# Attention in padded head pairs, fp32 transposes on TensorE, interleaved batches, and a hand-written TensorE order across two MoE layers

## The chip, the cores and the metric

The kernel runs on one core of a Trainium2 chip. The metric is device time in microseconds (us), the median of several runs. TensorE is PE in the profile (its weight loads PEld), VectorE is DVE, ScalarE is ACT, GpSimd is POOL, SyncE is SP. L171 is line 171 of the kernel concerned; before and after have their own numbers.

## What is computed

Four batches of 768 positions pass a linear attention with a decaying state per head (8 heads, 48 channels each), and its output, as x of 3072 x 384, a mixture of four experts in which every expert sees every row.

```python
for t in range(S):
    kt, vt, rt = (k[:, :, t].copy(), v[:, :, t].copy(), r[:, :, t].copy())
    cur = np.einsum('bhd,bhe->bhde', u[None] * kt, vt)
    y[:, :, t] = np.einsum('bhd,bhde->bhe', rt, state + cur)
    state = w[None, :, :, None] * state + np.einsum('bhd,bhe->bhde', kt, vt)
...
p = domain_probs / (domain_probs.sum(-1, keepdims=True) + 1e-09)
for e in range(E):
    h = np.maximum(x @ w1[e], 0.0)
    out += p[:, e:e + 1] * (h @ w2[e])
```

r, k, v, w and u are fp32, w1 is 4 x 384 x 1024 and w2 4 x 1024 x 384; the output is fp32.

## The kernel before

The work is cut into 24 chunks of 128 positions, six per batch, batch after batch. For a chunk `attn_chunk` (L118 to L191) loads r, k and v with positions on partitions (SP's queue, L126 to L128, three buffers each). VectorE multiplies r and k by powers of the decay into bf16 (L131, L133). GpSimd makes Khat, k scaled for the state (L135), Vb, v in bf16 (L137), the two products r·k·u (L140, L141), and, when VectorE has summed them per head (dcoef, L143), dv, the part of the position itself (L145).

TensorE transposes r and k head by head, 8 + 8 bf16 transposes of 48 columns (L149, L155), which VectorE copies out of PSUM (L151, L157). A per head is a product over 48 rows (L164); VectorE masks it to the triangle in two halves (AtM, L166). Y is, per head, AtM times Vb over 128 positions and r times the state over 48 rows, in turns (L171, L173). VectorE adds dv (Ysb, L176). The state's increment St is Khat times Vb per head (L180), after which VectorE decays the state and adds (L182, L184). Three transposes (L189) and a copy (L191) bring the chunk's Y, with its 384 channels on partitions, into xTe, which holds four chunks.

The MoE takes groups of four chunks. For each of 6 groups and 4 experts, 24 slots in all, layer 1 has 8 blocks of 128 hidden units, three matmuls of 512 columns each (L229), which ScalarE rectifies into hTs (L234); layer 2 has four blocks, one per chunk, of 8 matmuls of 384 columns (L238). VectorE scales a block by the expert's weight into tmp (L242), and GpSimd adds it to the accumulator oacc (L244), which it has cleared (L221). Four output DMAs on SP's queue follow a group (L248).

Six chunks are issued ahead of the MoE, then one at the start of every slot until they are used up (`issue_chunk`). The weights come in two DMAs of 3 MB each on GpSimd's queue, issued after the first chunk. Within this order of issue a scheduler decides how the instructions lie on each engine. PSUM has two buffers for transposes and A (tag trps), two for Y and St, two for layer 1 and two for layer 2.

## Time and profile before

| | us |
|---|---|
| runs | 437.08, 436.20, 436.51; median 436.51 |
| the profiled execution: span | 435.5 |
| TensorE busy | 370.9 (85%), 2568 matmuls |
| GpSimd busy | 215.9 (50%) |
| VectorE busy | 205.9 (47%) |
| ScalarE busy | 122.0 (28%) |
| moved by DMA | 25.62 MB |

The span runs from the first to the last thing that the profile shows on the core; the runs' time holds about 1 us more. A group in the profile is named by line, engine, operation, and what it writes from what, with its count, its busy time, the mean ns of one, and after the second bar the idle time of the engine just before these instructions with what ended it. In a timeline a row begins with start and duration in us, and a row of several instructions gives the time from the start of the first to the end of the last. In the rows of 40 slices a slice is 10.9 us and a digit is the busy share in tenths.

### The profile page before, as it was taken

Reading aid. Unit: us, or ns where it says so; the run is one execution under the profiler, and the core shown is the slowest. Engines: PE = TensorE matmul, PEld = TensorE weight load, DVE = VectorE, ACT = ScalarE, POOL = GpSimd, SP = SyncE. Lnnn points to the kernel's source line nnn. Section 1 sums busy time; section 2 is a strip of 40 time slices with the busy share of each in tenths; the row PEclk is TensorE's granted clock in tenths of the full one; section 3 lists DMA queues with packets and bytes.
Section 4 is the critical chain, followed back from the end, with each engine's and each line's share of the span. In section 5 each row is a group of like instructions: output and inputs, shape, how many; then the busy total and the mean of one; then the engine's idle time right before and its main releaser. Section 6 shows DMA issues by size and latency. Waiting matters only on the chain.

```text
span 435.5 us, 6346 instructions
## 1 busy us (share of the span) xinstructions
PE 370.9 (85%) x2568; PEld 209.6 (48%) x2568; DVE 205.9 (47%) x375; ACT 122.0 (28%) x202; POOL 215.9 (50%) x253
## 2 busy tenths in 40 slices
PE   0102357999999998999989999999999999999995
PEld 0101245565555554555545555555555555444442
DVE  1423357678765535456545535664544352222222
ACT  5100000121232241241332324133413334434441
POOL 2422859496774564654655565554433223343333
PEclk9999999999999998999999999999999999999999
DMA  7599995332421230120331122200001000020002
GB/s 103 71 199 196 187 185 116 78 72 52 93 47 27 74 90 20 37 56 20 90 75 36 36 40 54 74 1 2 0 2 38 36 2 0 2 73 2 0 2 72
DMA packets 87520, 25.62 MB, mean 59 GB/s; under 512 B 78786, under 2 KB 85956, under 8 KB 87492
## 3 DMA queue, kind: packets, MB, share of 16 engines
q1 hardware_dynamic: 81828, 18.93, 21.7%
q0 software_dynamic: 5664, 6.29, 8.5%
q8 instruction: 20, 0.33, 0.3%
q14 instruction: 8, 0.07, 0.1%
HBM read 26.79 MB, written 4.72 MB: 72 GB/s over the span
## 4 chain that ended last, share of the span: by engine, by line
PE 56%; DMA 16%; POOL 13%; issue 8%; DVE 6%; ACT 1%; POOLq 0%; DVEq 0%; ACTq 0%; SPq 0%
PE out_ps L238 22%; PE hT_ps L229 19%; DMA Kt<-in_k_dram 10%; DMA Rt<-in_r_dram 4%; PE Y_ps L173 4%; PE Y_ps L171 3%; POOL oacc L244 3%; POOL ruk L140 3%; POOL Khat L135 3%; POOL ruk L141 3%; DMA out_dram<-oacc 2%; PE RsT_ps L149 2%; DVE tmp L242 2%; PE KsT_ps L155 2%; PE At_ps L164 2%
## 5 line engine op out<-in xcount | busy, mean ns | idle before, releaser
L234 ACT ACTIVATE hTs<-hT_ps 128x512 bf16<-128x512 f32 x192 | 114.5, 597 | 291.7 <-PE hT_ps L229 287.3
L229 PE MATMUL hT_ps<-xTe,w_sb 128*128 128x512 bf16 x576 | 150.5, 382 | 0.9 <-ACT hTs L234 0.4
L238 PE MATMUL out_ps<-w_sb,hTs 128*128 128x384 bf16 x768 | 142.9, 329 | 4.5 <-DVE tmp L242 3.6
L244 POOL TENSOR_TENSOR oacc<-oacc,tmp 128x384 f32<-128x384 f32 x96 | 91.1, 954 | 104.3 <-DVE tmp L242 104.2
L242 DVE TENSOR_SCALAR tmp<-out_ps,p_nat 128x384 bf16<-128x384 f32 x96 | 58.7, 615 | 99.0 <-PE out_ps L238 98.9
L238 PEld LDWEIGHTS <-hTs 128*128 128x128 bf16 x768 | 73.5, 98 | 65.2 <-issue 8.5
L229 PEld LDWEIGHTS <-w_sb 128*128 128x128 bf16 x576 | 50.8, 97 | 55.5 <-issue 10.4
L171 PE MATMUL Y_ps<-Vb,AtM 128*128 128x48 bf16 x192 | 38.2, 199 | 21.6 <-DVE AtM L166 21.1
L135 POOL TENSOR_TENSOR Khat<-Kt,W_sd 128x384 bf16<-128x384 f32 x24 | 24.1, 1006 | 38.8 <-PE St_ps L180 38.8
L173 PE MATMUL Y_ps<-stateB,RsT 48*128 48x48 bf16 x192 | 37.9, 197 | 0.0
L145 POOL TENSOR_TENSOR dv<-Vt,dcoef 128x384 f32<-128x384 f32 x24 | 25.2, 1051 | 24.3 <-DVE dcoef L143 22.0
L176 DVE TENSOR_TENSOR Ysb<-Y_ps,dv 128x384 bf16<-128x384 f32 x24 | 13.4, 557 | 47.8 <-PE Y_ps L173 47.8
L149 PE MATMUL RsT_ps<-ident,Rs 128*48 128x128 bf16 x192 | 17.2, 240 | 19.8 <-DVE Rs L131 19.8
L171 PEld LDWEIGHTS <-AtM 128*128 128x128 bf16 x192 | 18.7, 98 | 31.1 <-DVE AtM L166 24.0
L166 DVE TENSOR_TENSOR AtM<-At_ps,mask 128x512 bf16<-128x512 f32 x48 | 30.7, 678 | 3.9 <-PE At_ps L164 3.9
L140 POOL TENSOR_TENSOR ruk<-Rt,Kt 128x384 f32<-128x384 f32 x24 | 24.3, 1014 | 15.3 <-DMA Kt<-in_k_dram 15.3
L143 DVE TENSOR_REDUCE dcoef<-ruk 128x8 f32<-128x384 f32 x24 | 13.0, 545 | 36.0 <-POOL ruk L141 36.0
L141 POOL TENSOR_TENSOR ruk<-ruk,U_sd 128x384 f32<-128x384 f32 x24 | 25.3, 1053 | 1.5
L149 PEld LDWEIGHTS <-Rs 128*48 128x48 bf16 x192 | 12.7, 113 | 26.0 <-DVE Rs L131 19.8
L173 PEld LDWEIGHTS <-RsT 48*128 48x128 bf16 x192 | 18.1, 94 | 13.3 <-issue 7.3
L131 DVE TENSOR_TENSOR Rs<-Rt,W_sd 128x384 bf16<-128x384 f32 x24 | 14.4, 600 | 17.0 <-DMA Rt<-in_r_dram 17.0
L164 PE MATMUL At_ps<-RsT,KsT 48*128 48x128 bf16 x192 | 16.7, 234 | 5.9 <-DVE KsT L157 5.9
(48 smaller groups left out, 201.7 us busy)
## 6 DMA issues: line engine op xcount, KB each, us to landing
w_sb<-in_moe_w_dram POOLq DMA_DIRECT2D x2, 3072.0 KB, 29.1
Rt<-in_r_dram SPq DMA_DIRECT2D x24, 192.0 KB, 3.4
Kt<-in_k_dram SPq DMA_DIRECT2D x24, 192.0 KB, 2.7
Vt<-in_v_dram SPq DMA_DIRECT2D x24, 192.0 KB, 3.0
out_dram<-oacc SPq DMA_DIRECT2D x24, 192.0 KB, 1.9
p_nat<-in_moe_domain_probs_dram SPq DMA_DIRECT2D x1, 48.0 KB, 3.8
w_row<-in_w_dram SPq DMA_DIRECT2D x1, 1.5 KB
u_row<-in_u_dram SPq DMA_DIRECT2D x1, 1.5 KB
```

The costliest lines, as they stand in the source:

```text
L135: nc.gpsimd.tensor_mul(Khat, Kt, W3_sd)
L140: nc.gpsimd.tensor_mul(ruk, Rt, Kt)
L141: nc.gpsimd.tensor_mul(ruk, ruk, U_sd)
L149: nc.tensor.transpose(RsT_ps[:, h, :], Rs[:, h, :], ident)
L166: nc.vector.tensor_mul(AtM[:, g * 4:(g + 1) * 4, :], At_ps, mask[:, None, :].to_broadcast((128, 4, C)))
L171: nc.tensor.matmul(Y_ps[:, h, :], AtM[:, h, :], Vb[:, h, :], start=True, stop=False)
L173: nc.tensor.matmul(Y_ps[:, h, :], RsT[:, h, :], stateB[:, h, :], start=False, stop=True)
L229: nc.tensor.matmul(hT_ps.rearrange("p a b -> p (a b)"), w1_sb[:, e, db, fb * 128:(fb + 1) * 128], xTe[:, db, :, :].rearrange("p a b -> p ( ...
L234: nc.scalar.activation(hTs[:, fb, :, :], hT_ps, AF.Relu)
L238: nc.tensor.matmul(out_ps, hTs[:, fb, s, :], w2_sb[:, e, fb, :], start=(fb == 0), stop=(fb == NFB - 1))
L242: nc.vector.tensor_scalar(tmp, out_ps, scalar1=p_nat[:, ci, e:e + 1], scalar2=None, op0=ALU.mult)
L244: nc.gpsimd.tensor_add(oacc[s], oacc[s], tmp)
```

## The change

The attention is laid out anew, and TensorE's and GpSimd's instructions stand in an order written out by hand.

*Layout.* Heads are padded from 48 to 64 channels, so that two of them fill 128 partitions. r and k are loaded into padded fp32 tiles (six buffers each) whose pads are zeroed once. TensorE transposes pairs straight from the loaded fp32 tile with an fp32 identity, 4 + 4 transposes per chunk (L191, L201); VectorE multiplies by the decay tables W1T and W2T, which ScalarE has built for the transposed layout, on the way out of PSUM (L195, L205). In the list of instructions such a transpose is one matmul row, where a bf16 matmul has a row for its weight load ahead of it. A is 8 matmuls over 64 rows, at rows 0 or 64 (L212). The state is block-diagonal for a pair, so Y has four matmuls of 96 columns with the state (L229, none for a batch's first chunk) and eight of 48 columns with Vb (L236), and St has four of 96 columns (L250, none for a batch's last chunk). GpSimd multiplies the state by the decay (two of 64x192, L259), VectorE adds the increment (L261).

*Order of chunks.* Chunk ci is position block ci//4 of batch ci%4, so four successive chunks belong to four batches and make up one MoE group.

*PSUM and buffers.* One buffer (tag tr) serves the transposes of r, of k and of Y; one of two banks holds A; one Y and St (tag ys); four hold the blocks of both MoE layers. Kh has three buffers, Vb four, hTs three, oacc twelve.

*MoE.* VectorE scales a layer-2 block into oacc (first expert, L298) or scales and adds in one instruction (L300). An output DMA follows each finished chunk (L303).

*Weights.* Eight DMAs on GpSimd's queue, one per expert and layer: the first expert's at the beginning, the others' after the attention work of chunks 1, 2 and 3 on that queue.

*Order on TensorE.* Chunks 0 to 3 come first, with the first expert on their group done chunk by chunk (96 matmuls of 128 columns). Then 23 slots each have 8 layer-1 blocks of their own, the 4 layer-2 blocks of the slot before, and attention steps in between: twelve steps (two chunks) in each of the first two slots, then six (one chunk) per slot while chunks last. The steps of chunk n are R (transposes of r), K, A, and those of n-1 lie between them: R(n), Y(n-1), K(n), St(n-1), A(n), x(n-1). VectorE, ScalarE and SP are still ordered by the scheduler.

VectorE near the start, before: what stands from the dcoef of chunk 4 (512) to the transposed r of chunk 3 (433); AtM_355 and Ysb_385 are chunk 2.

```order
L143 TENSOR_REDUCE dcoef_512<-ruk_509 128x8
L166 TENSOR_TENSOR AtM_355<-At_ps_356,mask_78 128x512
L166 TENSOR_TENSOR AtM_355<-At_ps_362,mask_78 128x512
L131 TENSOR_TENSOR Rs_592<-Rt_586,W1_sd_101 128x384
L176 TENSOR_TENSOR Ysb_385<-Y_ps_368,dv_331 128x384
L182 TENSOR_TENSOR stateB_125<-stateB_125,wCT_110 48x384
L191 COPY xTe0_126<-xT_ps_398 128x3x128
L184 TENSOR_TENSOR stateB_125<-stateB_125,St_ps_387 48x384
L151 COPY RsT_433<-RsT_ps_424 48x1024
```

The same place after: dcoef_732, 822 and 922 are chunks 5, 6 and 7; RsT_688, KsT_700, AtM_722 and Ysb_769 are chunk 4, RsT_749 is chunk 5.

```order
L183 TENSOR_REDUCE dcoef_732<-ruk_731 128x8
L195 TENSOR_TENSOR RsT_688<-RT_ps_683,W1T_149 128x512
L205 TENSOR_TENSOR KsT_700<-KT_ps_695,W2T_150 128x512
L183 TENSOR_REDUCE dcoef_822<-ruk_821 128x8
L298 TENSOR_SCALAR oacc_711<-out_ps_702,p_nat_163 128x384
L218 TENSOR_TENSOR AtM_722<-At_ps_713,mask_127 128x512 x2
L195 TENSOR_TENSOR RsT_749<-RT_ps_744,W1T_149 128x512
L183 TENSOR_REDUCE dcoef_922<-ruk_921 128x8
L240 TENSOR_TENSOR Ysb_769<-Y_ps_756,dv_672 128x384
```

Before, the dcoef of two chunks on stands ahead of a chunk's AtM, and none between AtM and Ysb; now the dcoef of two chunks on stands ahead of AtM and that of three chunks on ahead of Ysb.

VectorE in the middle of the program, before: RsT_1449 to Ysb_1492 are chunk 10, Rs_1967 is chunk 13, dcoef_2531 chunk 16.

```order
L151 COPY RsT_1449<-RsT_ps_1440 48x1024
L157 COPY KsT_1460<-KsT_ps_1451 48x1024
L131 TENSOR_TENSOR Rs_1967<-Rt_1961,W1_sd_101 128x384
L133 TENSOR_TENSOR Ks_1969<-Kt_1962,W2_sd_104 128x384
L166 TENSOR_TENSOR AtM_1462<-At_ps_1463,mask_78 128x512
L166 TENSOR_TENSOR AtM_1462<-At_ps_1469,mask_78 128x512
L176 TENSOR_TENSOR Ysb_1492<-Y_ps_1475,dv_1438 128x384
L182 TENSOR_TENSOR stateB_125<-stateB_125,wCT_110 48x384
L184 TENSOR_TENSOR stateB_125<-stateB_125,St_ps_1494 48x384
L191 COPY xTe2_1046<-xT_ps_1505 128x3x128
L143 TENSOR_REDUCE dcoef_2531<-ruk_2528 128x8
L242 TENSOR_SCALAR tmp_1560<-out_ps_1551,p_nat_115 128x384
```

After: AtM_2046 and Ysb_2130 are chunk 14, xT_ps_2065 is chunk 13, RsT_2099 and KsT_2153 are chunk 15, dcoef_2384 is chunk 17.

```order
L183 TENSOR_REDUCE dcoef_2384<-ruk_2383 128x8
L218 TENSOR_TENSOR AtM_2046<-At_ps_2037,mask_127 128x512 x2
L298 TENSOR_SCALAR oacc_2063<-out_ps_2054,p_nat_163 128x384
L268 COPY xTe_1914<-xT_ps_2065 128x3x128
L195 TENSOR_TENSOR RsT_2099<-RT_ps_2094,W1T_149 128x512
L298 TENSOR_SCALAR oacc_2110<-out_ps_2101,p_nat_163 128x384
L240 TENSOR_TENSOR Ysb_2130<-Y_ps_2117,dv_1929 128x384
L298 TENSOR_SCALAR oacc_2146<-out_ps_2137,p_nat_163 128x384
L205 TENSOR_TENSOR KsT_2153<-KT_ps_2148,W2T_150 128x512
L261 TENSOR_TENSOR S2_0_180<-S2_0_180,St_ps_2166 64x4x48 x2
```

The dcoef of a chunk three or more ahead stood behind xTe; now it stands ahead of AtM, and AtM and a layer-2 eviction ahead of xTe and of the RsT that follows it in the same PSUM buffer.

GpSimd in the middle, before: Khat_1971 and dv_1980 are chunk 13, ruk_2528 chunk 16.

```order
L135 TENSOR_TENSOR Khat_1971<-Kt_1962,W3_sd_107 128x384
L137 CAST Vb_1973<-Vt_1963 128x384
L145 TENSOR_TENSOR dv_1980<-Vt_1963,dcoef_1978 128x384
L140 TENSOR_TENSOR ruk_2528<-Rt_2514,Kt_2515 128x384
L141 TENSOR_TENSOR ruk_2528<-ruk_2528,U_sd_89 128x384
L244 TENSOR_TENSOR oacc0_1411<-oacc0_1411,tmp_1560 128x384
L244 TENSOR_TENSOR oacc1_1412<-oacc1_1412,tmp_1572 128x384
L244 TENSOR_TENSOR oacc2_1413<-oacc2_1413,tmp_1584 128x384
L244 TENSOR_TENSOR oacc3_1414<-oacc3_1414,tmp_1596 128x384
```

After: Kh1_86 and dv_2235 are chunk 16, Vb_2382 to Kh2_87 chunk 17, and S3_0 is the state of chunk 15's batch.

```order
L182 TENSOR_TENSOR Kh1_86<-Kt4_83,W3_sd_159 128x8x48
L184 TENSOR_TENSOR dv_2235<-Vt_1483,dcoef_2234 128x384
L259 TENSOR_TENSOR S3_0_182<-S3_1_183,wC_161 64x4x48 x2
L178 CAST Vb_2382<-Vt_1635 128x384
L179 TENSOR_TENSOR ruk_2383<-Rt5_78,Kt5_84 128x384
L180 TENSOR_TENSOR ruk_2383<-ruk_2383,U_sd_109 128x384
L182 TENSOR_TENSOR Kh2_87<-Kt5_84,W3_sd_159 128x8x48
```

The adds into oacc are gone, state products have come, and the products of the next chunk stand behind Kh and the state products of the ones before.

The diff, cut to the steps of the attention and the order that the prediction speaks of:

```diff
+    def pre(ci):
+        Rt, Kt, Vt = RtB[ci % NIN], KtB[ci % NIN], Vts[ci]
+        Kh = KhB[ci % 3]
...
+        if ci // B < NCH - 1:
+            nc.gpsimd.tensor_mul(Kh[:, :, 0:D], Kt[:, :, 0:D], W3_sd)
...
+    def stR(ci):
+        s = st[ci]
+        ps = psum.tile([128, NP, C], F32, tag="tr", bufs=1, name="RT_ps")
+        for q in range(NP):
+            nc.tensor.transpose(ps[:, q, :],
+                                s["Rt"][:, 2 * q:2 * q + 2, :].rearrange("p a b -> p (a b)"),
+                                ident_f)
+        s["RsT"] = work.tile([128, NP, C], BF16, tag="RsT", name="RsT")
+        nc.vector.tensor_mul(s["RsT"], ps, W1T)
...
+                nc.tensor.matmul(ps[:, j, q, :],
+                                 s["KsT"][j * P2:(j + 1) * P2, q, :],
+                                 s["RsT"][j * P2:(j + 1) * P2, q, :],
                                  start=True, stop=True)
...
+                nc.tensor.matmul(ps[:, 2 * q:2 * q + 2, :].rearrange("p a b -> p (a b)"),
+                                 s["RsT"][:, q, :], S_now[:, q, :],
+                                 start=first, stop=False, skip_group_check=True)
...
+                nc.gpsimd.tensor_mul(S_new[pr, :, cl], S_now[pr, :, cl],
+                                     wC[pr, :, None].to_broadcast((P2, NP, D)))
+                nc.vector.tensor_add(S_new[pr, :, cl], S_new[pr, :, cl], ps[pr, :, cl])
...
+            nc.vector.scalar_tensor_tensor(oaccs[ci], in0=ps, scalar=pe, in1=oaccs[ci],
+                                           op0=ALU.mult, op1=ALU.add)
...
+    with tc.manual_schedule(engines={ET.PE, ET.Pool}):
...
+        late = {4: [lambda: load_w1(1)], 9: [lambda: load_w2(1)],
+                15: [lambda: load_w1(2), lambda: load_w2(2)],
+                21: [lambda: load_w1(3), lambda: load_w2(3)]}
...
+        for si, (e, sc) in enumerate(slots):
+            rate = 3 if si < 2 else 1.5
+            for q in range(4):
+                for half in range(2):
+                    l1(e, sc, 2 * q + half, 0, SUB)
+                    carry += rate / 3
+                    while carry >= 1:
+                        carry -= 1
+                        f = next(steps, None)
+                        if f:
+                            f()
+                if prev:
+                    prev.pop(0)()
```

## Prediction

> **What bounds the kernel now.** The first view is the page. TensorE (PE) is busy in 85% of the span, and its row over 40 slices of 10.9 us says where it is not.

> ```profile
> span 435.5 us, 6346 instructions
> PE 370.9 (85%) x2568; PEld 209.6 (48%) x2568; DVE 205.9 (47%) x375; ACT 122.0 (28%) x202; POOL 215.9 (50%) x253
> ...
> PE   0102357999999998999989999999999999999995
> ...
> GB/s 103 71 199 196 187 185 116 78 72 52 93 47 27 74 90 20 37 56 20 90 75 36 36 40 54 74 1 2 0 2 38 36 2 0 2 73 2 0 2 72
> ...
> w_sb<-in_moe_w_dram POOLq DMA_DIRECT2D x2, 3072.0 KB, 29.1
> ...
> Kt<-in_k_dram SPq DMA_DIRECT2D x24, 192.0 KB, 2.7
> ```

> Up to about 80 us PE is half idle or more, and there the transfers run at 185 to 199 GB/s; afterwards PE is full. The chain of waits shows by name what the start waits for: two chunk loads that take 16 us, where the page has 2.7 us as the median of such a load.

> ```profile
> 19.81 15.70 DMA Rt<-in_r_dram
> 44.14 16.00 DMA Kt<-in_k_dram
> ```

> The loads share the way with 2 x 3072 KB of weights. So before is two stages: about 80 us bound by bytes, then 355 us bound by PE and what it waits for in each slot (one expert on one group of four chunks). PE's timeline prices the second stage. The first columns are start and duration; a group of n pipelined matmuls lasts one duration plus n-1 spacings.

> ```profile
> 228.19 2.76 PE L238 MATMUL out_ps<-w_sb,hTs 128*128 128x384 bf16 x16 [1.24 <-DVE tmp L242]
> 230.88 0.63 PE L149 MATMUL RsT_ps<-ident,Rs 128*48 128x128 bf16 x8
> 231.35 0.61 PE L155 MATMUL KsT_ps<-ident,Ks 128*48 128x128 bf16 x8
> ...
> 233.08 0.62 PE L164 MATMUL At_ps<-RsT,KsT 48*128 48x128 bf16 x8
> 233.63 1.04 PE L229 MATMUL hT_ps<-xTe,w_sb 128*128 128x512 bf16 x4
> ...
> 234.78 0.19 PE L173 MATMUL Y_ps<-stateB,RsT 48*128 48x48 bf16 x1
> 234.91 0.20 PE L171 MATMUL Y_ps<-Vb,AtM 128*128 128x48 bf16 x1
> ...
> 235.67 0.38 PE L180 MATMUL St_ps<-Vb,Khat 128*48 128x48 bf16 x8
> 235.98 0.39 PE L229 MATMUL hT_ps<-xTe,w_sb 128*128 128x512 bf16 x1
> ...
> 245.91 0.63 PE L149 MATMUL RsT_ps<-ident,Rs 128*48 128x128 bf16 x8
> ...
> 364.43 2.36 PE L229 MATMUL hT_ps<-xTe,w_sb 128*128 128x512 bf16 x9
> ...
> 375.35 2.36 PE L229 MATMUL hT_ps<-xTe,w_sb 128*128 128x512 bf16 x9
> ```

> A slot with a chunk of attention takes 245.91 - 230.88 = 15.03 us, one without 375.35 - 364.43 = 10.92. Spacings: 512 columns (1.04 - 0.39)/3 = 0.217; 384 columns (2.76 - 0.33)/15 = 0.162; 128 columns (231.35 - 230.88)/8 = 0.059. L171 and L173, which change between 128 and 48 rows each time, stand 0.13 apart, the eight equal ones of L180 0.31/8 = 0.039.

> **The change: PE's work.** A slot's MoE stays 24 x 0.217 + 32 x 0.162 = 10.4 us, 24 slots 249.6. Layer 2 of the slot before now lies among layer 1, so I take 10.4 and not the 10.92 that a slot without attention takes now; if that mixing brings nothing, 24 x 0.52 = 12 us come back.

> Attention per chunk: 16 bf16 transposes become 8 in fp32, which no row shows. The list of instructions has one matmul row for each and no row for a weight load ahead of it, so nothing can be loaded early. I take load and one pass in series.

> ```profile
> L238 PEld LDWEIGHTS <-hTs 128*128 128x128 bf16 x768 | 73.5, 98 | 65.2 <-issue 8.5
> ```

> A load takes 98 ns, a pass 0.059: 0.157 each. [...] Eight are 1.26 us. A, eight matmuls of 64 rows: 8 x 0.059 and two changes of rows, 0.65 (now 233.08 to 233.63 is 0.55). Y, twelve matmuls that all use 128 rows: between L180's 0.039 and a 128-column pass, say 0.05: 0.60; St 4 x 0.05 = 0.20; x 3 x 0.059 = 0.17. Sum 2.88, times 24 = 69, less 1.6 for the state matmuls that the first chunks of a batch lack and the St that the last lack: 67.5. With 0.4 for the 96 small matmuls of the first group (0.059 against 0.217/4 each), PE has 317.5 us to do, where it was busy for 370.9.

> **The start.** Transfers set it.

> ```profile
> 22.00:65.00 43.00, 12.92 (x105) 9.66 (x106) 16.28 (x29) 0.00 (x0) 20.48 (x26) 1.00 1.18 192
> ```

> The last column is 192 GB/s. Up to chunk 6 there are 6.29 MB of weights (all of them are asked for by then), 7 x 0.59 of inputs and some 0.4 of tables: 10.8 MB, 56.4 us, plus 2 for the first issue, 58.4; chunk 7 61.5. Chunk 7 counts, because in the new order VectorE's dcoef of chunk 6 stands ahead of AtM of chunk 4, and that of chunk 7 ahead of Ysb of chunk 4. How long GpSimd takes per chunk comes from its groups, those of VectorE beside it (busy time and mean ns of one).

> ```profile
> L244 POOL TENSOR_TENSOR oacc<-oacc,tmp 128x384 f32<-128x384 f32 x46 | 45.6, 1001 | 20.0 <-DVE tmp L242 19.8
> L141 POOL TENSOR_TENSOR ruk<-ruk,U_sd 128x384 f32<-128x384 f32 x13 | 13.1, 1011 | 1.0
> L140 POOL TENSOR_TENSOR ruk<-Rt,Kt 128x384 f32<-128x384 f32 x13 | 12.9, 995 | 10.6 <-DMA Kt<-in_k_dram 10.6
> L135 POOL TENSOR_TENSOR Khat<-Kt,W_sd 128x384 bf16<-128x384 f32 x12 | 11.9, 993 | 28.5 <-PE St_ps L180 28.5
> L145 POOL TENSOR_TENSOR dv<-Vt,dcoef 128x384 f32<-128x384 f32 x12 | 11.8, 987 | 5.2 <-DVE dcoef L143 3.3 <-DVE Ysb L176 1.9
> L137 POOL CAST Vb<-Vt 128x384 bf16<-128x384 f32 x12 | 6.4, 530 | 1.0
> ...
> L242 DVE TENSOR_SCALAR tmp<-out_ps,p_nat 128x384 bf16<-128x384 f32 x46 | 27.8, 614 | 18.9 <-PE out_ps L238 18.8
> L166 DVE TENSOR_TENSOR AtM<-At_ps,mask 128x512 bf16<-128x512 f32 x26 | 16.6, 676 | 0.4 <-PE At_ps L164 0.4
> L143 DVE TENSOR_REDUCE dcoef<-ruk 128x8 f32<-128x384 f32 x15 | 8.1, 548 | 33.2 <-POOL ruk L141 33.2
> L176 DVE TENSOR_TENSOR Ysb<-Y_ps,dv 128x384 bf16<-128x384 f32 x12 | 6.7, 557 | 25.7 <-PE Y_ps L173 25.7
> L191 DVE COPY xTe<-xT_ps 128x384 bf16<-128x384 bf16 x12 | 4.1, 343 | 0.0
> ```

> From 58.4: Vb and two products of chunk 6 to 60.9, Khat, dv and two state products to 64, Vb and two products of chunk 7 to 66.6, then dcoef and Ysb: 68. The state products (2 x 64x192, bf16) have no row; half the elements of Khat bound them below at 0.5, a whole Khat above at 1.0; I take 0.55.

> By 68 PE has done the first slot but for a quarter of layer 2 (5.6 + 3.9), that quarter (1.3), six layer-1 blocks (3.9), chunks 0 to 3 (4 x 2.7), chunk 4 (2.5) and the transposes of chunk 5 (1.3): 29.3. Left are 288. Start 6 us either way.

> **The new wait.** From then on, VectorE's order ties PE to GpSimd. St of chunk n-1 on PE frees the buffer of Kh, of which there are three; GpSimd then makes Kh and dv of n+2 and the state products, and Vb and two products of n+3: 0.99 + 0.99 + 1.1 + 0.53 + 1.0 + 1.01 = 5.62 us. VectorE has dcoef of n+3 ahead of AtM of n, a layer-2 eviction and xTe of n-1: 0.55 + 1.27 + 0.61 + 0.34 = 2.77. Only xTe frees the one PSUM buffer (tag tr) that the R transposes of n+1 need. With seven handovers of 0.07 (below, GpSimd starts at 431.22, VectorE's 0.62 from 430.53 ends at 431.15) the way round is 8.9 us. Between this St and that R, PE has in its order three stretches of 4/3 layer-1 and 2/3 layer-2 blocks (1.73 us each), A, x and St: 6.2 us. It waits 2.7. A slot with one chunk then takes 10.4 + 2.9 + 2.7 = 16.0, more than the 15.03 of now. Twelve chunks (8 to 19; the last four have no Kh) give 32, and the two slots with two chunks each, where PE has about half as much in between, an estimated 6: 38. What hides the rest of GpSimd (5.6 us per 16) and of VectorE (four evictions 2.4, dcoef, AtM, Ysb and xTe 2.7, two transposed tiles and two state adds at L166's and L176's prices 2.4: 7.5 per slot) is PE's slot itself.

> **The end.** VectorE's last eviction starts 435.5 - 430.53 = 5.0 us before the end.

> ```profile
> 430.53 0.62 DVE L242 TENSOR_SCALAR tmp<-out_ps,p_nat 128x384 bf16<-128x384 f32 x1 [0.68 <-PE out_ps L238]
> 431.22 0.91 POOL L244 TENSOR_TENSOR oacc<-oacc,tmp 128x384 f32<-128x384 f32 x1 [0.39 <-DVE tmp L242]
> ```

> GpSimd's add and its handover, 0.98, go, since VectorE adds while it evicts (taken as L242's 0.61), so with 0.1 ahead of the eviction 4.1 us follow PE. The other adds cost nothing now: GpSimd waits for tmp before them, 19.8 us in the stretch shown, and nobody for it.

> **Sum.** 68 + 288 + 38 + 4 = 398 of span. The profiled execution has a span of 435.5 and the median of the runs is 436.5; the 1.0 around the span stays: 399.

> **Rivals.** *The loop doesn't bind*: GpSimd runs ahead, or PE's own work in between is nearer 9 us. For it: GpSimd is 50% busy now and loses the adds, 45.6 of the 180 us shown. Against: three Kh buffers tie it to PE's St, as Khat waits 28.5 us for St even now. Without the 38, 361.

> [...]

> [...] No operation in fp32 runs on PE in the trace of before.

> [...]

> *GpSimd's feed is dearer*: state products at 1.0 add 0.9 per chunk over some 14 chunks, 13 us; a GpSimd 10% slower beside VectorE adds 8: 412 to 420.

> *A longer start*: one more load of 16 us as in the chain: 415. For it: eight weight transfers in the queue instead of two; against: three quarters of them are issued later than now.

> **How the numbers follow.** Forecast 0.61, no loop 0.09, four passes 0.05, four loads and passes 0.10, dearer feed 0.10, longer start 0.05. The forecast's own range is 384 (transposes at 0.059: 160 x 0.098 = 16 less) to 424 (feed and slots of 10.92 together: 13 + 12 more). The 80% range, 381 to 430, leaves out no loop and four loads and passes, and reaches past 415 by the bounds on top. A change within 0.2% is about what a measurement of this kernel cannot tell from none: same 0.01. Slower is four loads and passes and a little for what I don't see, 0.11; faster 0.88.

> **What would show it.** Right: transposes 0.16 apart; slots of 16.0 in the middle, with PE idle before L191 put down to VectorE's xTe and GpSimd's Kh waiting for PE's St; PE full from about 68; slots of 10.4 at the end. Wrong: transposes 0.4 or more apart; no wait at L191; GpSimd without waits, which makes it the bound by itself; or PE empty beyond 75.

## The result, and the profile after

The changed kernel takes 407.78 us (median of four runs, 404.26 to 409.99) against 436.36 us before (four runs beside it, 434.57 to 437.08); the ratio is 0.9347, 95% interval 0.9287 to 0.9407. The forecast was 399, with a range of 381 to 430. The profiled execution has a span of 403.6 us.

The page of the changed kernel, its lines that answer to those of before (the last three are a group of GpSimd's, one of TensorE's and one of the DMA queue's; a slice is now 10.1 us):

```profile
span 403.6 us, 5634 instructions
...
PE 326.0 (81%) x2224; PEld 186.5 (46%) x2224; DVE 168.0 (42%) x328; ACT 123.2 (31%) x230; POOL 124.7 (31%) x176
...
PE   0156780868678979779798797799999999999996
...
PEclk9999997598999899998899898989999999999999
...
GB/s 126 133 171 186 193 193 183 175 116 57 43 39 60 88 49 40 22 39 41 97 58 41 39 22 19 47 52 2 1 2 20 60 0 2 0 60 19 2 0 78
...
L182 POOL TENSOR_TENSOR Kh<-Kt,W_sd 128x384 bf16<-128x384 f32 x20 | 20.0, 998 | 116.1 <-PE St_ps L250 114.0
L191 PE MATMUL RT_ps<-ident_f,Rt 128*128 128x128 f32 x96 | 17.7, 313 | 46.2 <-DVE xTe L268 33.5
...
w_sb<-in_moe_w_dram POOLq DMA_DIRECT2D x8, 768.0 KB, 12.9
```

TensorE is busy for a smaller share than before. It starts earlier, but from 60 to 280 us its row has sevens, and the granted clock (PEclk), which on the page of before has 9s and one 8, has a 7, a 5 and many 8s. In the start the 9s of this row are not to be trusted: the clock's first record stands at 40.7 us (before: 83.6), and four fp32 transposes take 1.11 us at 33.37 us and 0.60 at 54.51. The two groups name the two ends of the predicted loop: GpSimd's Kh waits for PE's St (114.0 us in all), and PE's R waits for VectorE's xTe (33.5 us).

PE's timeline in the middle of the program, two R transposes apart (start, duration):

```profile
228.25 0.99 PE L191 MATMUL RT_ps<-ident_f,Rt 128*128 128x128 f32 x4 [2.33 <-DVE xTe L268]
229.04 2.77 PE L293 MATMUL out_ps<-w_sb,hTs 128*128 128x384 bf16 x8
231.60 0.93 PE L280 MATMUL hT_ps<-xTe,w_sb 128*128 128x512 bf16 x3
...
233.38 1.46 PE L293 MATMUL out_ps<-w_sb,hTs 128*128 128x384 bf16 x8
234.69 0.60 PE L201 MATMUL KT_ps<-ident_f,Kt 128*128 128x128 f32 x4
235.12 1.46 PE L280 MATMUL hT_ps<-xTe,w_sb 128*128 128x512 bf16 x6
236.42 0.33 PE L250 MATMUL St_ps<-Vb,Kh 128*128 128x96 bf16 x4
...
238.63 0.40 PE L212 MATMUL At_ps<-RsT,KsT 64*128 64x128 bf16 x8
238.96 0.82 PE L280 MATMUL hT_ps<-xTe,w_sb 128*128 128x512 bf16 x3
...
244.89 0.66 PE L191 MATMUL RT_ps<-ident_f,Rt 128*128 128x128 f32 x4 [2.34 <-DVE xTe L268]
```

The wait stands where it was forecast, 2.33 us long. Four fp32 transposes take 235.12 - 234.69 = 0.43 us, 0.108 each. The slot takes 16.64 us. And something stands here that no step had: the eight layer-2 matmuls behind the wait take 2.77 us, those 4 us later 1.46. The trace in stretches of 1 us shows what it was (the figure before the last two is the granted clock):

```profile
229.00:230.00 1.00, 1.00 (x6) 0.46 (x4) 0.69 (x1) 0.00 (x0) 0.00 (x0) 0.50 0.00 0
...
231.00:232.00 1.00, 1.00 (x5) 0.48 (x4) 0.16 (x1) 0.00 (x0) 0.00 (x0) 0.58 0.38 75
232.00:233.00 1.00, 1.00 (x17) 0.65 (x16) 0.53 (x2) 0.43 (x1) 0.00 (x0) 1.00 0.00 0
```

After the wait PE runs at half clock for some 3.4 us and loses 1.7. Of the nine slots between 117 and 262 us six take 16.6 us and three 14.95; those three had the same wait and kept the clock (the last section sets the stops side by side). VectorE's timeline of that place shows what it stood at:

```profile
225.66 0.55 DVE L183 TENSOR_REDUCE dcoef<-ruk 128x8 f32<-128x384 f32 x1 [3.58 <-POOL ruk L180]
226.13 1.28 DVE L218 TENSOR_TENSOR AtM<-At_ps,mask 128x512 bf16<-128x512 f32 x2
227.32 0.61 DVE L300 SCALAR_TENSOR_TENSOR oacc<-out_ps,p_nat,oacc 128x384 f32<-128x384 f32 x1
227.85 0.35 DVE L268 COPY xTe<-xT_ps 128x384 bf16<-128x384 bf16 x1
```

It waits 3.58 us for GpSimd's product three chunks on; then AtM, an eviction and xTe, one behind another, and PE starts R at 228.25.

**Where the time came from.** The start of a slot's last layer-2 matmul, read from both timelines: slot 2 119.7 before and 106.6 after, slot 12 275.8 and 267.8, slot 18 364.3 and 342.2, slot 24 430.1 and 399.5. The first two slots give 13 us; in the ten that follow, with the loop, 5 are lost again; slots 13 to 18, where the loop has run out and a chunk costs PE 2 us where it cost nearly 4, give 14; the last six, without attention, 8.5. Together 30.6. (Layer 2 of a slot now ends within the next one, so all these times of after but the last stand some 5 us late in this count, which belongs to the first two slots and is given back at the end.)

### The profile page after: what moved, and what is told of

Its sections match the earlier page's. It is cut to its first block, busy times and chain, and to the rows that moved or that the text cites. A ratio compares the mean times of both kernels' runs of the same rounds, so it can differ in the third digit from the quotient of the medians.

```text
span 403.6 us, 5634 instructions
## 1 busy us (share of the span) xinstructions
PE 326.0 (81%) x2224; PEld 186.5 (46%) x2224; DVE 168.0 (42%) x328; ACT 123.2 (31%) x230; POOL 124.7 (31%) x176
## 3 DMA queue, kind: packets, MB, share of 16 engines
q0 software_dynamic: 5760, 6.29, 9.1%
## 4 chain that ended last, share of the span: by engine, by line
PE 50%; POOL 22%; DVE 10%; issue 8%; DMA 7%; SPq 1%; ACT 1%; POOLq 0%; ACTq 0%
PE out_ps L293 22%; PE hT_ps L280 20%; POOL ruk L180 5%; POOL ruk L179 5%; DMA Vt<-in_v_dram 4%; DVE AtM L218 4%; POOL Kh L182 4%; POOL S L259 3%; POOL dv L184 3%; PE RT_ps L191 3%; PE KT_ps L201 2%; DMA wT<-in_w_dram 2%; POOL Vb L178 2%; DVE oacc L300 2%; SPq L83 1%
## 5 line engine op out<-in xcount | busy, mean ns | idle before, releaser
L284 ACT ACTIVATE hTs<-hT_ps 128x512 bf16<-128x512 f32 (+1 forms) x216 | 116.5, 549 | 254.7 <-PE hT_ps L280 252.7
L280 PE MATMUL hT_ps<-xTe,w_sb 128*128 128x512 bf16 (+1 forms) x648 | 155.4, 372 | 0.0
L300 DVE SCALAR_TENSOR_TENSOR oacc<-out_ps,p_nat,oacc 128x384 f32<-128x384 f32 x72 | 44.4, 617 | 77.4 <-PE out_ps L293 77.3
L182 POOL TENSOR_TENSOR Kh<-Kt,W_sd 128x384 bf16<-128x384 f32 x20 | 20.0, 998 | 116.1 <-PE St_ps L250 114.0
L191 PE MATMUL RT_ps<-ident_f,Rt 128*128 128x128 f32 x96 | 17.7, 313 | 46.2 <-DVE xTe L268 33.5
L191 PEld LDWEIGHTS RT_ps<-ident_f,Rt 128*128 128x128 f32 x96 | 11.8, 156 | 55.6 <-DVE xTe L268 42.3
L201 PE MATMUL KT_ps<-ident_f,Kt 128*128 128x128 f32 x96 | 16.6, 301 | 12.7 <-DVE RsT L195 12.6
L298 DVE TENSOR_SCALAR oacc<-out_ps,p_nat 128x384 f32<-128x384 f32 x24 | 14.8, 617 | 24.7 <-PE out_ps L293 24.7
L180 POOL TENSOR_TENSOR ruk<-ruk,U_sd 128x384 f32<-128x384 f32 x24 | 23.8, 994 | 1.9
L195 DVE TENSOR_TENSOR RsT<-RT_ps,W1T 128x512 bf16<-128x512 f32 x24 | 16.6, 690 | 16.2 <-PE RT_ps L191 16.2
L201 PEld LDWEIGHTS KT_ps<-ident_f,Kt 128*128 128x128 f32 x96 | 12.6, 153 | 15.7 <-DVE RsT L195 14.2
L240 DVE TENSOR_TENSOR Ysb<-Y_ps,dv 128x384 bf16<-128x384 f32 x24 | 13.3, 556 | 13.1 <-PE Y_ps L236 12.8
L236 PE MATMUL Y_ps<-Vb,AtM 128*128 128x48 bf16 x192 | 10.1, 193 | 10.4 <-POOL dv L184 9.6
L205 DVE TENSOR_TENSOR KsT<-KT_ps,W2T 128x512 bf16<-128x512 f32 x24 | 16.4, 684 | 3.6 <-PE KT_ps L201 3.6
## 6 DMA issues: line engine op xcount, KB each, us to landing
w_sb<-in_moe_w_dram POOLq DMA_DIRECT2D x8, 768.0 KB, 12.9
Rt<-in_r_dram SPq DMA_DIRECT2D x24, 192.0 KB, 4.2
Kt<-in_k_dram SPq DMA_DIRECT2D x24, 192.0 KB, 3.9
Vt<-in_v_dram SPq DMA_DIRECT2D x24, 192.0 KB, 4.6
out_dram<-oacc SPq DMA_DIRECT2D x24, 192.0 KB, 1.8
logw_bc<-in_w_dram SPq DMA_DIRECT2D x1, 192.0 KB, 4.5
U_sd<-in_u_dram SPq DMA_DIRECT2D x1, 192.0 KB, 5.9
```

The costliest lines, as they stand in the source:

```text
L180: nc.gpsimd.tensor_mul(ruk, ruk, U_sd)
L182: nc.gpsimd.tensor_mul(Kh[:, :, 0:D], Kt[:, :, 0:D], W3_sd)
L191: nc.tensor.transpose(ps[:, q, :], s["Rt"][:, 2 * q:2 * q + 2, :].rearrange("p a b -> p (a b)"), ident_f)
L201: nc.tensor.transpose(ps[:, q, :], s["Kt"][:, 2 * q:2 * q + 2, :].rearrange("p a b -> p (a b)"), ident_f)
L280: nc.tensor.matmul(ps[:, 0:n, :].rearrange("p a b -> p (a b)"), w1_sb[:, e, db, fb * 128:(fb + 1) * 128], xTe[:, db, s0:s0 + n, :].rearran ...
L284: nc.scalar.activation(hTs[:, fb, s0:s0 + n, :], ps[:, 0:n, :], AF.Relu)
```

## The experiments

All leave nothing out of the computation. Each ratio is against the kernel before, with its 95% interval.

**1. More Kh buffers** (label kh6).

```diff
-    KhB = [inputs.tile([128, H, P2], BF16, name=f"Kh{i}") for i in range(3)]
+    KhB = [inputs.tile([128, H, P2], BF16, name=f"Kh{i}") for i in range(6)]
...
-        Kh = KhB[ci % 3]
+        Kh = KhB[ci % 6]
```

> Only the number of Kh buffers changes, 3 to 6. Theory A (the loop: St on PE frees Kh, GpSimd's feed, VectorE's dcoef ahead of AtM and xTe, then R on PE): GpSimd's Kh no longer waits for St, only Vb (four buffers) does, so the way round loses Kh, dv and the state products (about 3 us) and falls below PE's own 6.2 us. The wait of 2.3 us at R (L191) goes in most slots, and with it the stretches at half clock behind it: from 403.6 to 360-370 us. Rival B (R waits because one PSUM buffer tr serves R, K and x, whatever GpSimd does): the wait of 2.3 stays, 402-408.

Measured 368.54 us, ratio 0.845 (0.8395 to 0.8504). Waits of PE over the whole run:

```profile
PE RT_ps L191 <- DVE xTe L268: 8.8, 5, 3.4
```

33.5 us became 8.8, most slots 12.76 us. The loop goes through Kh; rival B falls.

**2. VectorE in the written order** (dve_written). Kh keeps its three buffers.

```diff
-    with tc.manual_schedule(engines={ET.PE, ET.Pool}):
+    with tc.manual_schedule(engines={ET.PE, ET.Pool, ET.DVE}):
```

> Only VectorE's order changes: it is the written one, too, so that dcoef of chunk n stands ahead of RsT of n and no longer ahead of AtM of n-3; all buffers as in the change. A: VectorE then never waits for products three chunks on, the loop is cut although Kh still has three buffers and GpSimd still waits for St; waits at L191 and half clock go, and the start no longer waits for the loads of chunks 6 and 7: 345-360. B: the wait at L191 stays and 400-408, less what the start gives.

Measured 349.75 us, ratio 0.8019 (0.7975 to 0.8062). PE's waits, its timeline from one R to the next, and the clock from 80 to 300 us:

```profile
PE RT_ps L191 <- DVE xTe L268: 1.5, 3, 1.2
```
```profile
208.67 0.60 PE L191 MATMUL RT_ps<-ident_f,Rt 128*128 128x128 f32 x4
209.10 1.46 PE L293 MATMUL out_ps<-w_sb,hTs 128*128 128x384 bf16 x8
...
211.05 0.33 PE L229 MATMUL Y_ps<-S,RsT 128*128 128x96 bf16 x4
211.22 0.36 PE L236 MATMUL Y_ps<-Vb,AtM 128*128 128x48 bf16 x8
211.43 0.81 PE L280 MATMUL hT_ps<-xTe,w_sb 128*128 128x512 bf16 x3
```
```profile
80.00:300.00 220.00, 217.93 (x1570) 127.91 (x1598) 119.38 (x219) 85.25 (x143) 77.92 (x105) 1.00 0.24 49
```

No wait, clock 1.00, 12.40 us a slot all through. So the loop needs both links, the buffer and dcoef's place ahead of AtM; taking either away cuts it. The second edit costs no memory and brings 58 us, more than the whole change, but it orders all of VectorE anew, so not all of that is dcoef's place: R of chunk 6 also starts at 72.66 in place of 79.48 us.

**3. Two PSUM buffers for tr** (tr2; three for the MoE blocks).

```diff
-        ps = psum.tile([128, NP, C], F32, tag="tr", bufs=1, name="RT_ps")
+        ps = psum.tile([128, NP, C], F32, tag="tr", bufs=2, name="RT_ps")
...
-        ps = psum.tile([128, SUB, 128], F32, tag="mm", bufs=4, name="hT_ps")
+        ps = psum.tile([128, SUB, 128], F32, tag="mm", bufs=3, name="hT_ps")
```

> The PSUM tag tr gets two buffers, the MoE blocks three in place of four. A: R no longer waits for xTe, but VectorE still stands at dcoef, so AtM, xTe and RsT are as late as before and PE waits for them one or two steps on, with 2 us more of cover: the wait falls to 0.5 us or moves to Y (AtM) or K: 370-390. B: the cause is gone, no wait in its place, 355-365.

Measured 383.42 us, ratio 0.8785 (0.8736 to 0.8834). PE and VectorE in a slot:

```profile
193.36 0.60 PE L191 MATMUL RT_ps<-ident_f,Rt 128*128 128x128 f32 x4
195.60 1.46 PE L293 MATMUL out_ps<-w_sb,hTs 128*128 128x384 bf16 x8 [1.64 <-DVE oacc L298]
```
```profile
193.28 0.55 DVE L183 TENSOR_REDUCE dcoef<-ruk 128x8 f32<-128x384 f32 x1 [3.59 <-POOL ruk L180]
```

R no longer waits, but VectorE stands at dcoef for 3.59 us as before, and PE now waits for the eviction that is queued behind it, at layer 2 and not, as I expected, at Y or K. The wait moved and shrank to 1.64; the cause is where VectorE stands.

**4 and 5. Work in the wait** (fill with ten matmuls, fill_half with five).

```diff
     def stR(ci):
         s = st[ci]
+        if 8 <= ci < 21:
+            fill = psum.tile([128, SUB, 128], F32, tag="mm", bufs=4, name="fill_ps")
+            for j in range(10):
+                nc.tensor.matmul(fill.rearrange("p a b -> p (a b)"), w1_sb[:, 0, 0, 0:128],
+                                 w1_sb[:, 0, 0, 0:512],
+                                 start=True, stop=True)
```

> Work is added: ahead of R of chunks 8 to 20 PE does ten matmuls of 512 columns (2.2 us) whose result nobody reads; nothing is left out. If the half clock follows the waits at L191: the wait of 2.3 falls to about 0.2, the clock stays at 1.0 in these slots, the nine stretches at half clock (1.7 us each) go, and the time falls to 387-393 although PE does 28 us more. If the clock falls by itself or with PE's load: 403-410, clock 0.94 or lower.

> As fill, with five matmuls of 512 columns (1.1 us) ahead of R of chunks 8 to 20 in place of ten; nothing left out. PE then stands still for about 1.25 us where it stood 2.33 in the change and 0.18 in fill. If the half clock needs a longer stop than about 1.25 us, the clock stays 1.0 in these slots, a slot takes 14.95 us as with fill, and the time is 393-398. If every stop brings it, slots stay at 14.95 or 16.6 by turns and the time is 402-408.

Measured 397.3 us, ratio 0.9113 (0.9061 to 0.9165), and 395.33 us, 0.9092 (0.9049 to 0.9136). The stretch 110 to 250 us of the change, of fill and of fill_half, and a wait in fill_half:

```profile
110.00:250.00 140.00, 118.96 (x790) 65.54 (x789) 60.43 (x113) 41.13 (x69) 45.72 (x62) 0.93 0.21 47
```
```profile
110.00:250.00 140.00, 137.41 (x929) 76.29 (x946) 63.67 (x121) 44.78 (x76) 51.79 (x70) 1.00 0.22 50
```
```profile
110.00:250.00 140.00, 127.72 (x883) 71.52 (x897) 64.26 (x121) 45.30 (x76) 50.57 (x69) 1.00 0.22 50
```
```profile
203.80 1.24 PE L192 MATMUL fill_ps<-w_sb 128*128 128x512 bf16 x5
206.30 0.66 PE L197 MATMUL RT_ps<-ident_f,Rt 128*128 128x128 f32 x4 [1.25 <-DVE xTe L274]
```

With PE busy for 18 us more in the stretch (fill) the kernel is faster: the clock is 1.00 and every slot 14.95 us. So here the clock fell with the stops (0.93 in the change), not with PE's load, and the stops of 1.25 us in fill_half did not bring it: its clock is 1.00 too. fill misses its 387 to 393: I had counted nine stretches of 1.7 us where the slots have six, and for chunks 8, 19 and 20 the fill is work that no full wait covers (2.9 us by the distances of their R from the one ahead, against the change).

**6. Weights later** (weights_later: expert 1 after chunk 2, 2 after 5, 3 after 7).

```diff
+            for e, after in ((1, 2), (2, 5), (3, 7)):
+                if state["pre"] == after + 1:
+                    load_w1(e)
+                    load_w2(e)
...
-        late = {4: [lambda: load_w1(1)], 9: [lambda: load_w2(1)],
-                15: [lambda: load_w1(2), lambda: load_w2(2)],
-                21: [lambda: load_w1(3), lambda: load_w2(3)]}
+        late = {}
```

> Nothing but the places of the weight loads on GpSimd's queue: expert 1 after chunk 2, expert 2 after chunk 5, expert 3 after chunk 7. If the start is set by the bytes ahead of chunk 6 (my step), 3.1 MB less stand ahead of it, 16 us at 192 GB/s, and PE's stop of 9.6 us at 61-71 us goes, with the half clock up to 82 us behind it (4 us): 404-408 falls to 390-397, R of chunk 6 starts at 63-70 us in place of 79.5. If the start is set by the order of VectorE and GpSimd alone, R of chunk 6 stays at 77-80 and the time at 402-409.

Measured 394.8 us (four runs, 391.09 to 397.47), ratio 0.9046 (0.8978 to 0.9113); R of chunk 6 at 69.98 us, and the clock is 1.00 from 40 until 118 us. VectorE's order, which the scheduler makes, moved a little with it (dcoef of chunk 7 now stands ahead of AtM of chunk 4, which is rather against a gain). The weights ahead of the early chunks set the end of the start. VectorE's order has a part in it too: R of chunk 6 starts at 72.66 us with the written order alone (experiment 2) and at 64.31 with both (experiment 8).

**7. domain_probs later** (probs_later). VectorE's scaling of the table (norm_p) moves behind the loads with them.

```diff
-        for _ in range(4):
+        for _ in range(3):
             load_next()
+        load_p()
+        load_next()
...
+            if i == 14:
+                norm_p()
```

> The six small loads of domain_probs go from ahead of chunk 1's loads on SP's queue to behind those of chunk 3. The bytes up to chunk 6 run at 126 and 133 GB/s in the first 20 us, not at my 192. If SP's 8.8 us on these small loads are the hole, loads of chunks 1 to 3 land up to 8 us earlier and the start shortens by 3-7 us: 397-404. If the weights in the queue behind set the end of the start all the same, nothing: 403-409.

Measured 409.5 us, ratio 0.9401 (0.9346 to 0.9456), no gain. Chunk 1's loads are issued at 10.7 in place of 19.3 us, but PE's R of chunk 1 starts at 25.20 as before, and R of chunk 6 at 78.96. The hole was not on the path.

**8. The written order and the later weights together** (written_and_weights).

> VectorE's written order (349.8 us) and the later weight loads together, nothing left out. The stop of 7.7 us before K of chunk 5 (at 58.8-66.5 us), where chunk 5's inputs wait behind weights, goes with the half clock behind it (2.8): 340-347. If PE's own order is what remains, 348-350.

Measured 342.41 us, ratio 0.788 (0.7838 to 0.7921): the stop before K of chunk 5 is 0.43 us.

**9 and 10. Is it the mixing of the layers?** Both stand on 8. layers_apart undoes the mixing; apart_split also splits the shared PSUM buffers in two and two.

```diff
+            own = [lambda e=e, sc=sc, s=s: l2(e, sc, s) for s in range(SUB)]
...
-                if prev:
-                    prev.pop(0)()
+            for q in range(4):
+                own[q]()
```
```diff
-        ps = psum.tile([128, SUB, 128], F32, tag="mm", bufs=4, name="hT_ps")
+        ps = psum.tile([128, SUB, 128], F32, tag="mm1", bufs=2, name="hT_ps")
...
-        ps = psum.tile([128, Dm], F32, tag="mm", bufs=4, name="out_ps")
+        ps = psum.tile([128, Dm], F32, tag="mm2", bufs=2, name="out_ps")
```

> On the kernel with VectorE's written order and later weights (342.4 us), the mixing of the layers is undone: a slot does its eight layer-1 blocks, then its own four layer-2 blocks, with as many attention steps as before. My step took 10.4 us for a mixed slot in place of the 10.92 that unmixed ones took before: if the mixing gives that, 23 x 0.52 = 12 us come back, 350-356. If the four PSUM buffers that the layers now share are what made the slots 10.4, nothing comes back: 339-346.

> On layers_apart (339.7 us) the four PSUM buffers that both layers share become two for layer 1 and two for layer 2, as before the change. If these buffers are why a slot without attention takes 10.4 us and took 10.92, slots grow by about 0.5 us each, 12 us in all: 349-353. If they are not, 339-342.

Measured 339.67 us, ratio 0.7816 (0.7785 to 0.7848), the lowest of all (against 8 the intervals touch), and 349.12 us, 0.8029 (0.7988 to 0.8069). A pure slot of each, from layer 1 to the next layer 1:

```profile
291.94 5.34 PE L280 MATMUL hT_ps<-xTe,w_sb 128*128 128x512 bf16 x24
297.12 5.36 PE L293 MATMUL out_ps<-w_sb,hTs 128*128 128x384 bf16 x32
302.31 5.34 PE L280 MATMUL hT_ps<-xTe,w_sb 128*128 128x512 bf16 x24
```
```profile
288.11 6.00 PE L280 MATMUL hT_ps<-xTe,w_sb 128*128 128x512 bf16 x24
293.94 5.36 PE L293 MATMUL out_ps<-w_sb,hTs 128*128 128x384 bf16 x32
299.14 6.00 PE L280 MATMUL hT_ps<-xTe,w_sb 128*128 128x512 bf16 x24
```

Unmixed, a slot still takes 10.37 us; with two buffers per layer 11.03, all of it in layer 1 (5.18 against 5.83 us). What a slot without attention gains is the number of buffers that layer 1 can use. The mixing gives nothing here.

**11. k's transposes twice** (k_twice, on 8).

```diff
-        for q in range(NP):
+        for q in list(range(NP)) * 2:
             nc.tensor.transpose(ps[:, q, :],
                                 s["Kt"][:, 2 * q:2 * q + 2, :].rearrange("p a b -> p (a b)"),
```

> On the same kernel the four fp32 transposes of k are done twice, the second over the first; work is added, none is left out. PE is the bound there, so the difference is the price of 4 x 24 transposes, of which about 4 x 19 lie outside the transfer-bound start: at the 0.108 us at which they stand in the trace +8 to 10 (350-354), at my 0.157 +12 to 15, at four passes (0.236) +18 to 23, at four loads and passes (0.63) +48.

Measured 353.06 us, ratio 0.8125 (0.809 to 0.8161): 10.7 more than 8, and a slot takes 12.83 in place of 12.40 us. 0.43/4 = 0.108 each, as in the trace.

**12. Two tr buffers on 8** (written_weights_tr2).

> On the same kernel tag tr gets two buffers and the MoE blocks three. What is left of waits at L191 (3.2 us in all, near the start) goes: 339-342. If three MoE buffers are too few for VectorE's written order, PE waits at layer 2 as it did with tr2 (1.6 us a slot): 350-365.

Measured 343.92 us, ratio 0.7926 (0.7884 to 0.7969), no difference from 8. The waits at L191 are gone and others of the same size stand in the start instead.

## Why the prediction was right, and where not

The time lies 9 us above the forecast, the direction as told, and the loop with it. Set against the steps, for the profiled execution:

| step | predicted | measured |
|---|---|---|
| until Ysb of chunk 4 is out | 68 | 75.5 |
| PE's work from there, at full clock | 288 | 277 |
| waits of PE | 38 | 31 |
| half clock | 0 | 16 |
| after PE | 4 | 3.8 |
| span | 398 | 403.6 |

Two steps were 18 us too dear together and two 24 us too cheap, so that the sum came this near is in part luck. The measured waits are L191's after 76 us (30.8) and K's (0.6). The half clock is worked out from two stretches; between them and behind them the clock is 1.00:

```profile
76.00:110.00 34.00, 25.99 (x186) 14.45 (x184) 16.91 (x34) 7.76 (x13) 16.70 (x23) 0.87 0.52 88
...
130.00:300.00 170.00, 149.16 (x996) 83.01 (x997) 76.91 (x145) 51.45 (x87) 52.45 (x70) 0.93 0.17 39
```

34 x 0.13 + 170 x 0.07 = 16.3, and PE's work is what is left of 399.8 - 75.5.

**The loop: right.** Its place, its links and its size came out: the wait is 2.33 us for 2.7, the way round from St to R 244.89 - 236.42 = 8.47 for 8.9, and PE's own work in between 6.13 for 6.2. Experiments 1 and 2 cut it at two different links, and 3 shows that the PSUM buffer alone is not the cause. That the slots take 16.07 us on the mean of the nine, for 16.0, is luck: a chunk costs PE less than forecast, and the half clock, which was not forecast, fills the gap.

**PE's work: the terms were mis-sized.** "A load takes 98 ns, a pass 0.059: 0.157 each" is 0.108 (experiment 11). What failed there is "so nothing can be loaded early": load and pass are not in series, as the last section shows. A, 0.65 with "two changes of rows", is 238.96 - 238.63 = 0.33 in the timeline above. "Y, twelve matmuls" at 0.05 each are 211.43 - 211.05 = 0.38 in experiment 2's timeline, not 0.60. Attention per chunk is 12.40 - 10.4 = 2.0, not 2.9. Each chunk was too dear by 0.9, 17 us over 19 chunks, which would leave 271 of the 288 where 277 were measured. Of the 6 between, 2.6 stand in the twelve slots of the loop (14.95 is 0.2 more than 12.40 and the wait of 2.33); the rest I can't place. No run shows the 0.236 or 0.63 (four passes, four loads and passes) that the chances and experiment 11's expectation also count with: at these it would have read +18 or +48, and it read +10.7.

**The start: failed in a step.** "6.29 MB of weights (all of them are asked for by then)" at 192 GB/s from the beginning. The weights of experts 1 to 3 are asked for only when GpSimd gets there:

```profile
32.21 0.81 POOL L98 DMA_DIRECT2D w_sb<-in_moe_w_dram  x1
...
39.82 0.81 POOL L98 DMA_DIRECT2D w_sb<-in_moe_w_dram  x1
...
46.92 0.81 POOL L98 DMA_DIRECT2D w_sb<-in_moe_w_dram  x1
...
66.51 0.50 POOL L178 CAST Vb<-Vt 128x384 bf16<-128x384 f32 x1 [8.06 <-DMA Vt<-in_v_dram]
```

From 32.2 us 4.7 MB of them and two chunks of 0.59 MB are to come: 31 us at 192 GB/s, 63, and chunk 6's v lands at 66.5. A sum of bytes needs the time at which they are asked for. That weights stand ahead of the early chunks, and not SP's small loads, is shown by 6 and 7. Of its own signs for being wrong the prediction touched one here, PE empty beyond 75: the last stop of the start ends at 75.53 us.

**The half clock: not in any step.** I read 0.99 in the rows of before and took it for the rest. The wait that I predicted costs 2.3 us, and in two of three slots another 1.7. It goes with the spread of the runs: 404.26 and 409.99 us are three to four such slots apart, and the granted clock on record is 0.953 in the first and 0.931 in the second. Which slots were halved in them is not shown, since they left no traces.

**10.92 or 10.4: right number, wrong reason.** The prediction gave it to the mixing; 9 and 10 give it to the buffers.

## What to carry to other kernels

## What the runs showed of the hardware

Why did equal stops not have equal effects? In the changed kernel PE stands still for 3.73 us ahead of R at 91.15 and again at 103.93 us. Behind the first the granted clock is 0.50 from 91.89 to 95.30 us, behind the second it stays 1.00. In rows as long as this half clock, 3.41 us, with one row on it, the first stop fills two rows, the second the last two (the first busy time is PE's; the figure before the last two is the granted clock):

```profile
85.06:88.48 3.42, 2.36 (x20) 1.16 (x14) 1.29 (x2) 1.04 (x2) 3.28 (x6) 1.00 0.80 154
88.48:91.89 3.41, 0.74 (x6) 0.62 (x7) 1.39 (x4) 0.00 (x0) 1.16 (x2) 1.00 0.00 0
91.89:95.30 3.41, 3.41 (x22) 1.82 (x21) 1.20 (x2) 0.60 (x1) 0.00 (x0) 0.50 0.30 60
...
98.71:102.13 3.42, 1.50 (x11) 0.66 (x8) 0.61 (x2) 0.60 (x1) 3.20 (x6) 1.00 0.29 58
102.13:105.54 3.41, 1.61 (x20) 1.24 (x21) 2.03 (x4) 0.27 (x1) 0.37 (x1) 1.00 0.00 0
```

The first leaves PE idle for 3.41 - 0.74 = 2.67 us of the row ahead of the half clock. The second is split, 1.92 and 1.80, and the clock stays. So it is with the stops of 2.33 us in this trace, in rows of 3.41 us counted back from the next half clock: in the six slots that lost the clock the row ahead of the half clock holds 2.01 to 2.34 us of idle PE, in the three others the stop is split so that no row holds more than 1.95. fill_half shows both sides: behind its stop of 2.67 us, which ends at 101.91, the clock is 0.50 for 3.4 us from 102.4; behind one of 3.74 us, which ends at 90.7, it stays 1.00, and in rows counted back from 102.4 that stop is split into 1.79 and 1.95. That the place of a stop decides is my reading of these two traces; no run moved a stop alone to test it.

An fp32 transpose of 128x128 without a load row of its own stands 0.108 us from the next; the profile still shows a load for each, and load and matmul overlap, since either lasts longer than the distance (156 and 313 ns in the mean):

```profile
L191 PEld LDWEIGHTS RT_ps<-ident_f,Rt 128*128 128x128 f32 x96 | 11.8, 156 | 55.6 <-DVE xTe L268 42.3
```
